# Splitting the first value product of a fused attention and SwiGLU kernel over two one-bank PSUM tiles

## The chip, the cores and the metric

The kernel runs on one core of a Trainium2 chip. A core has five engines that run side by side: PE (matrix products; PEld is its weight load), DVE (vector), ACT (scalar and activation), POOL (general purpose) and SP, which issues the DMA transfers. PE writes into PSUM, eight banks of 2 KB per partition; DVE and ACT read PSUM, all engines work on SBUF. The metric is the device time of one execution in microseconds (us), lower is better. It is given as the median of the runs; one further execution was taken with the hardware profiler and is the source of every trace row here.

## The reference

Memory attention followed by a SwiGLU feed-forward layer, in float32 (weights arrive as float64):

```python
a = softmax(phi, axis=2)                       # 8 batches, 8 heads, 576 tokens, 32 memories
k_m = einsum('bhsm,bhsd->bhmd', a, k)
v_m = einsum('bhsm,bhsd->bhmd', a, v)
attn = softmax(q @ k_m.T / 8)
x = (attn @ v_m) -> (4608, 512)                # heads side by side
xn = x / sqrt(mean(x*x) + 1e-6) * rms_g
out = (silu(xn @ w_gate) * (xn @ w_val)) @ w_out     # 512 -> 1536 -> 512
```

## The kernel before

Precision is kept by splitting a float32 operand into a rounded high part and the rest (names ending in h and l), and adding three products: high x high, high x low, low x high. A split is one ACT CAST (high) and one subtraction (low) on DVE or POOL.

The first part (until about 148 us) reduces phi, k and v to memories, computes the attention of the first two pairs of batches, and begins to convert the weights from float64. A conversion is six DVE instructions on a 128x512 tile (lines L345, L365, L347, L369, L358, L385, which write the tiles ex, mi and at last w), two ACT passes between them (L350 for ex, L376 for mi), then an ACT CAST to wh or oh (L402) and a subtraction on POOL to wl or ol (L403). A name like ex2_0 is kind 2 (w_out) of block 0; kinds 0 and 1 are w_gate and w_val.

The second part is 48 steps i, one for each pair of batches and block of 128 columns of the hidden layer. Attention and value memories are not multiplied out: each step computes

- the value product vp: the pair's value memories times the block of w_gate and w_val, 12 matmuls 128x256 (L840), in one PSUM tile with tag vw, two banks, one buffer; index cc is 0 or 1, the pair of heads;
- its evacuation: xh (ACT, L853) and xl (DVE, L854), each in two halves of 64 partitions, the second with its two blocks swapped;
- the gate and value products pg and pv (L876): xh and xl times the attention weights ath and atl, for four groups of columns, with tags g and v, two banks each;
- sg = silu(pg) on ACT (L884), hf = pv x sg on DVE (L885), the split of hf into hh (ACT) and hl (POOL);
- after every second step, the output products po (L918), 9 times 6 matmuls 128x512, tag o, two banks, added to acc on DVE (L925; the first time copied by ACT, L923).

Beside them run the conversion of the remaining weights and the attention of the last two pairs (query transposes qtp, scores S), whose PSUM tiles are also of tag o.

The order of the work: each helper returns a list of closures, each is given a number (the tables VW, GV, O, PRE, PSW, SU and others), and they are recorded in the order of the numbers. The recorded program then goes through the language's own scheduler, which reorders each engine's instructions by its own estimate of their times and sets the waits. So a small edit in one step can move instructions in later ones. The second part takes over the PSUM banks from the first; a tile waits until the last reader of its banks in the first part is done.

Of the kernel before, what the change touches and what calls it, by code (L numbers as in the profile page):

```python
# [8 lines left out]
F32 = mybir.dt.float32  # L9
# [4 lines left out]
ALU = mybir.AluOpType  # L14
# [76 lines left out]
def kernel(  # L91
# [25 lines left out]
    nc = tc.nc  # L117
    P = 128
# [309 lines left out]
    with ExitStack() as c1:  # L428
        sb = c1.enter_context(tc.tile_pool(name="sb1", bufs=2, reuse_waits="tile"))
        ps = c1.enter_context(tc.tile_pool(name="ps1", bufs=2, space=PSUM, reuse_waits="tile"))  # L430
# [330 lines left out]
        def place(base, offsets, steps):  # L761
            assert len(offsets) == len(steps)
            return [(base + o, f) for o, f in zip(offsets, steps)]
# [8 lines left out]
        for b in range(B):  # L772
# [11 lines left out]
            else:  # L784
                p0 = PRM["PH"][b - 2] + PRM["PD"][b - 2]
                ev += place(p0, PRM["PREP"], preps[b][:5])
                e = max(K_AT[b - 2] + 6 * PRM["KP"], p0 + PRM["PREP"][-1]) + PRM["EXP"][b - 2]
# [3 lines left out]
        for pr in range(G):  # L791
            for s in range(HP):
                t = PRM["S_AT"][pr * HP + s]
# [18 lines left out]
    sb = ctx.enter_context(tc.tile_pool(name="sb2", bufs=1, reuse_waits="tile"))  # L812
    ps = ctx.enter_context(tc.tile_pool(name="ps2", bufs=2, space=PSUM, reuse_waits="tile"))

    NS = (NP // G) * NU * G * 2
    vw, hsplit, accs = {}, {}, {}

    def where(i):

        ps_, r = divmod(i, NU * G * 2)  # L820
        u, r = divmod(r, G * 2)
        pi, f = divmod(r, 2)
        return ps_, u, ps_ * G + pi, 2 * u + f

    def vw_steps(i):

        ps_, u, pr, j = where(i)

        def mm(cc):
            def f():  # L830
                if cc == 0:
                    vw[i] = [ps.tile([P, 2, 2, 256], F32, tag="vw", name=f"vp{i}", bufs=1)]
                vp = vw[i][0]
                vh, vl = vm[pr][:, 0], vm[pr][:, 1]
                wh, wl = (x.rearrange("p hp g f -> p hp (g f)") for x in wsplit[ps_ * NJ + j])
                for e in range(2):
                    def lhs(vt):
                        return vt[:, cc, e].rearrange("p o x -> p (o x)")
                    for n, (l, r) in enumerate(((vh, wh), (vh, wl), (vl, wh))):
                        nc.tensor.matmul(  # L840
                            vp[:, cc, e, :], lhs(l), r[:, 2 * cc + e, :],
                            start=(n == 0), stop=(n == 2),
                        )
            return f

        def evac():
            vp = vw[i][0]
            xh = sb.tile([P, 2, 2, 256], F32R, tag="xh", name=f"xh{i}", bufs=2)
            xl = sb.tile([P, 2, 2, 256], F32R, tag="xl", name=f"xl{i}", bufs=2)
            for h in range(2):  # L850
                rows = slice(64 * h, 64 * h + 64)
                src = vp[rows, :, ::-1, :] if h else vp[rows]
                nc.scalar.copy(xh[rows], src)  # L853
                nc.vector.tensor_tensor(out=xl[rows], in0=src, in1=xh[rows].bitcast(F32), op=ALU.subtract)  # L854
            vw[i] = xh, xl
        return [mm(0), mm(1), evac]
# [78 lines left out]
    def o_tile(name):  # L935
        return ps.tile([P, 512], F32, tag="o", name=name)
# [104 lines left out]
    ev = place(-1.0, PRM["VW"], vw_steps(0))  # L1041
    for i in range(NS):
        ps_, u, pr, j = where(i)
        ev += place(i, PRM["GV"], gv_steps(i))
        if i + 1 < NS:
            ev += place(i + (PRM["VW0"] if i == 0 else 0), PRM["VW"], vw_steps(i + 1))
# [59 lines left out]
```

## Time and profile before

| | |
|---|---|
| median of 3 runs | 908.6 us (907.46 to 909.01) |
| the profiled execution, its own time | 910.09 us |
| its span, first to last instruction | 908.3 us |
| granted PE clock over the span | 0.969 |
| PE busy | 838.9 us (92%) |
| DVE busy | 592.2 us (65%) |
| ACT busy | 421.1 us (46%) |
| POOL busy | 286.6 us (32%) |

The shares are means over stages with different limits, so the prediction cuts the span into stretches. In rows of the order of time, a group of alike instructions is one row with its start and length; the brackets tell how long the engine sat idle before it and what ended that.

### The profile page before, as it was taken

How to read it: one execution, taken by the hardware profiler on the slowest of the kernel's cores; microseconds unless marked ns; L12 is line 12 of the kernel's file. 1: busy time of each engine (PE TensorE's matmuls, PEld its weight loads, DVE VectorE, ACT ScalarE, POOL GpSimd, SP SyncE). 2: the span in 40 equal slices, each digit the busy share in tenths (PEclk: the TensorE clock that was granted, in tenths of full speed). 3: DMA queues.
4: the chain of work that ended last, by engine and by line, in shares of the span. 5: the costliest groups of instructions: out<-in, count | busy, mean ns of one | idle time of the engine just before them, and what ended most of it. 6: DMA issues, size and time to landing. Idle time of an engine off the chain costs nothing.

```text
span 908.3 us, 15828 instructions
## 1 busy us (share of the span) xinstructions
PE 838.9 (92%) x6207; PEld 744.3 (82%) x6207; DVE 592.2 (65%) x1026; ACT 421.1 (46%) x717; POOL 286.6 (32%) x242
## 2 busy tenths in 40 slices
PE   4989485899989999899999999999999999999997
PEld 3777474889887899788888997798889999999996
DVE  5577968997898877988754655632445455454543
ACT  2656433777766464665543343254424333243330
POOL 3463745333333324234242241412112121121120
PEclk9889887999999999999999999999999999999999
DMA  8976543553464341634214134411204012040046
GB/s 284 324 254 236 201 157 96 182 185 86 153 166 132 106 119 61 165 110 153 89 58 140 35 94 128 97 55 47 93 1 140 1 48 93 1 140 1 1 111 144
DMA packets 81506, 106.41 MB, mean 117 GB/s; under 512 B 34324, under 2 KB 52248, under 8 KB 81432
## 3 DMA queue, kind: packets, MB, share of 16 engines
q1 hardware_dynamic: 81432, 105.41, 37.6%
q8 instruction: 49, 0.80, 0.4%
q14 instruction: 25, 0.20, 0.1%
HBM read 73.93 MB, written 31.46 MB: 116 GB/s over the span
## 4 chain that ended last, share of the span: by engine, by line
PE 74%; DVE 14%; issue 4%; DMA 4%; ACT 3%; POOL 1%; SPq 0%; DVEq 0%; ACTq 0%; POOLq 0%
PE po L918 29%; PE pv L876 14%; PE pg L876 14%; PE vp L840 7%; PE kvp L573 3%; PE xp L235 1%; DVE mi L365 1%; DVE xl L854 1%; DVE ex L345 1%; DVE w L385 1%; ACT xh L853 1%; PE qtp L685 1%; DVE mi L369 1%; DVE acc L925 1%; DMA phi<-in_phi_dram 1%
## 5 line engine op out<-in xcount | busy, mean ns | idle before, releaser
L899 POOL TENSOR_TENSOR hl<-hf,hh 128x512 fp32r<-128x512 f32 (+1 forms) x96 | 139.6, 1454 | 410.9 <-ACT hh L898 399.6
L925 DVE TENSOR_TENSOR acc<-po,acc 128x512 f32<-128x512 f32 x180 | 123.1, 687 | 130.2 <-PE po L918 129.5
L918 PE MATMUL po<-oh,hh 128*128 128x512 f32 x432 | 173.6, 403 | 3.6 <-DVE acc L925 2.6
L918 PE MATMUL po<-oh,hl 128*128 128x512 f32 x432 | 171.1, 396 | 0.0
L918 PE MATMUL po<-ol,hh 128*128 128x512 f32 x432 | 170.9, 396 | 0.0
L884 ACT ACTIVATE sg<-pg 128x256 f32<-128x256 f32 x192 | 77.7, 409 | 163.2 <-PE pg L876 144.2
L854 DVE TENSOR_TENSOR xl<-vp,xh 64x1024 fp32r<-64x1024 f32 x96 | 117.2, 1220 | 45.9 <-ACT xh L853 44.4
L885 DVE TENSOR_TENSOR hf<-pv,sg 128x256 f32<-128x256 f32 x192 | 85.3, 453 | 73.0 <-PE pv L876 51.1
L853 ACT CAST xh<-vp 64x1024 fp32r<-64x1024 f32 x96 | 96.6, 1007 | 51.7 <-PE vp L840 21.6
L898 ACT CAST hh<-hf 128x512 fp32r<-128x512 f32 (+1 forms) x96 | 64.6, 673 | 82.3 <-DVE hf L885 57.0
L918 PEld LDWEIGHTS po<-oh,hl 128*128 128x128 f32 x432 | 81.5, 189 | 19.5
L918 PEld LDWEIGHTS po<-oh,hh 128*128 128x128 f32 x432 | 81.5, 189 | 19.3 <-DVE acc L925 4.5
L876 PE MATMUL pg<-ath,xh 128*128 128x320 f32 (+1 forms) x384 | 86.6, 299 | 7.9 <-ACT xh L853 6.3
L918 PEld LDWEIGHTS po<-ol,hh 128*128 128x128 f32 x432 | 81.7, 189 | 11.5 <-DMA ol<-od 0.2
L840 PE MATMUL vp<-wh,vm 128*128 128x256 f32 x384 | 85.5, 288 | 4.8 <-DVE at L212 2.3
L876 PE MATMUL pv<-ath,xh 128*128 128x320 f32 (+1 forms) x384 | 84.7, 300 | 4.7 <-DVE hf L885 4.6
L876 PE MATMUL pg<-ath,xl 128*128 128x320 f32 (+1 forms) x384 | 85.7, 296 | 0.0
L876 PE MATMUL pv<-atl,xh 128*128 128x320 f32 (+1 forms) x384 | 84.7, 296 | 0.0
L876 PE MATMUL pg<-atl,xh 128*128 128x320 f32 (+1 forms) x384 | 84.4, 297 | 0.0
L876 PE MATMUL pv<-ath,xl 128*128 128x320 f32 (+1 forms) x384 | 83.3, 296 | 0.0
L876 PEld LDWEIGHTS pg<-ath,xh 128*128 128x128 f32 x384 | 63.8, 190 | 13.3 <-ACT xh L853 6.6
L840 PEld LDWEIGHTS vp<-wh,vm 128*128 128x128 f32 x384 | 66.0, 191 | 8.4 <-DVE xl L854 3.0
(129 smaller groups left out, 1377.5 us busy)
## 6 DMA issues: line engine op xcount, KB each, us to landing
kv<-in_k_dram SPq DMA_DIRECT2D x32, 288.0 KB, 4.8
kv<-in_v_dram SPq DMA_DIRECT2D x32, 288.0 KB, 5.4
out_dram<-acc SPq DMA_DIRECT2D x72, 128.0 KB, 2.4
raw<-in_moe_w_gate_dram SPq DMA_DIRECT2D x12, 512.0 KB, 4.8
raw<-in_moe_w_val_dram SPq DMA_DIRECT2D x12, 512.0 KB, 3.7
wd<-wh SPq DMA_DIRECT2D x12, 512.0 KB, 3.0
wd<-wl SPq DMA_DIRECT2D x12, 512.0 KB, 4.1
raw<-in_moe_w_out_dram SPq DMA_DIRECT2D x12, 512.0 KB, 3.6
```

Source lines behind the costliest of these rows:

```text
L235: nc.tensor.matmul(xp[64 * j:64 * j + 64, P * cc:P * cc + P], st["at"][:, t, cc, 64 * j:64 * j + 64], gb[:, j, cc], start=True, stop=True,)
L573: nc.tensor.matmul(kvp[64 * par:64 * par + 64, cc, 0:128], e_bd[j][:, hp, c, :], st["kv", b, hp][:, :, 64 * c:64 * c + 64], start=(c == 0) ...
L840: nc.tensor.matmul(vp[:, cc, e, :], lhs(l), r[:, 2 * cc + e, :], start=(n == 0), stop=(n == 2),)
L853: nc.scalar.copy(xh[rows], src)
L854: nc.vector.tensor_tensor(out=xl[rows], in0=src, in1=xh[rows].bitcast(F32), op=ALU.subtract)
L876: nc.tensor.matmul(pt[:, :N], l[:, cc, b, half * P:half * P + P], r[:, b, cc, t0:t0 + n, :].rearrange("p t x -> p (t x)"), start=(m == 0), ...
L884: nc.scalar.activation(sg[:, :N], pg[:, :N], AF.Silu)
L885: nc.vector.tensor_tensor(out=hf[:, :, b, :], in0=pv[:, :N].rearrange("p (t x) -> p t x", x=64), in1=sg[:, :N].rearrange("p (t x) -> p t x ...
L898: nc.scalar.copy(hh, hv)
L899: nc.gpsimd.tensor_tensor(out=hl, in0=hv, in1=hh.bitcast(F32), op=ALU.subtract)
L918: nc.tensor.matmul(po, l[:, tt, :], r, start=(m == 0), stop=(m == 5))
L925: nc.vector.tensor_tensor(out=accs[key], in0=po, in1=accs[key], op=ALU.add)
```

## The change

For step 0 alone, the value product is written into two tiles of one bank each, one for each cc, with tag o (the output products' banks). Each tile is evacuated by itself: two CASTs of 64x512, then two subtractions of 64x512. All later steps keep the two-bank tile. Three tiles that nothing uses are created first, so that tags vw, v and g keep banks ahead of o.

```diff
+    ps.tile([P, 2, 2, 256], F32, tag="vw", name="vw_first", bufs=1)
+    for t in "vg":
+        ps.tile([P, 512], F32, tag=t, name=f"{t}_first")
...
         def mm(cc):
             def f():
-                if cc == 0:
-                    vw[i] = [ps.tile([P, 2, 2, 256], F32, tag="vw", name=f"vp{i}", bufs=1)]
-                vp = vw[i][0]
+                if i == 0:
+                    vw.setdefault(i, []).append(o_tile(f"vp{i}_{cc}").rearrange("p (e f) -> p e f", e=2))
+                elif cc == 0:
+                    whole = ps.tile([P, 2, 2, 256], F32, tag="vw", name=f"vp{i}", bufs=1)
+                    vw[i] = [whole[:, 0], whole[:, 1], whole]
+                vp = vw[i][cc]
...
-                            vp[:, cc, e, :], lhs(l), r[:, 2 * cc + e, :],
+                            vp[:, e, :], lhs(l), r[:, 2 * cc + e, :],
...
         def evac():
-            vp = vw[i][0]
             xh = sb.tile([P, 2, 2, 256], F32R, tag="xh", name=f"xh{i}", bufs=2)
             xl = sb.tile([P, 2, 2, 256], F32R, tag="xl", name=f"xl{i}", bufs=2)
+            if i == 0:
+                for cc, vp in enumerate(vw[i]):
+                    halves = ((slice(0, 64), vp[:64]), (slice(64, P), vp[64:, ::-1, :]))
+                    for rows, src in halves:
+                        nc.scalar.copy(xh[rows, cc], src)
+                    for rows, src in halves:
+                        nc.vector.tensor_tensor(
+                            out=xl[rows, cc], in0=src, in1=xh[rows, cc].bitcast(F32), op=ALU.subtract
+                        )
+                vw[i] = xh, xl
+                return
+            vp = vw[i][2]
             for h in range(2):
```

In the built program the count of matmuls, DMAs and POOL instructions is unchanged; ACT has two CASTs more and DVE two subtractions more. The order differs from step 0's value product on; from step 15's gate product on it is the same again on every engine. Line numbers in the changed kernel are 5 to 20 higher.

Three places. In these rows a name carries its step or block and then a number of the program's own; x2 is two alike in a row. First ACT, just before and in step 0's evacuation: before,

```order
L350 ACTIVATE ex2_0_1828<-ex2_0_1828 128x512
L853 CAST xh0_1822<-vp0_1809 64x1024
L376 ACTIVATE mi2_0_1833<-mi2_0_1833 128x512
L853 CAST xh0_1822<-vp0_1809 64x1024
L402 CAST oh0_2027<-w2_0_1839 128x512
```

and now, up to the table load for silu:

```order
L862 CAST xh0_1826<-vp0_0_1812 64x512 x2
L350 ACTIVATE ex2_0_1836<-ex2_0_1836 128x512
L862 CAST xh0_1826<-vp0_1_1819 64x512 x2
L376 ACTIVATE mi2_0_1841<-mi2_0_1841 128x512
L402 CAST oh0_2035<-w2_0_1847 128x512
L873 CAST xh1_1901<-vp1_1849 64x1024
L904 ACT_TABLE_LOAD
```

The first tile's two CASTs moved ahead of ex2_0, and step 1's first CAST ahead of the table load. Second DVE at the same place: before,

```order
L369 SCALAR_TENSOR_TENSOR mi2_0_1833<-raw_20_1724,mi2_0_1833 128x512
L358 SCALAR_TENSOR_TENSOR ex2_0_1828<-raw_20_1724,ex2_0_1828 128x512
L854 TENSOR_TENSOR xl0_1823<-vp0_1809,xh0_1822 64x1024
L385 TENSOR_TENSOR w2_0_1839<-mi2_0_1833,ex2_0_1828 128x512
L345 TENSOR_SCALAR ex2_1_1969<-raw_21_1741 128x512
L365 TENSOR_SCALAR mi2_1_1980<-raw_21_1741 128x512
L854 TENSOR_TENSOR xl0_1823<-vp0_1809,xh0_1822 64x1024
```

and now:

```order
L369 SCALAR_TENSOR_TENSOR mi2_0_1841<-raw_20_1724,mi2_0_1841 128x512
L864 TENSOR_TENSOR xl0_1827<-vp0_0_1812,xh0_1826 64x512 x2
L358 SCALAR_TENSOR_TENSOR ex2_0_1836<-raw_20_1724,ex2_0_1836 128x512
L864 TENSOR_TENSOR xl0_1827<-vp0_1_1819,xh0_1826 64x512 x2
L385 TENSOR_TENSOR w2_0_1847<-mi2_0_1841,ex2_0_1836 128x512
```

The subtractions of the first tile stand ahead of ex2_0's last pass, those of the second ahead of w2_0. Third ACT again, at the silu of steps 1 and 2: before,

```order
L853 CAST xh2_1974<-vp2_1917 64x1024
L402 CAST wh2_2074<-w0_2_2068 128x4x128
L402 CAST wh2_2074<-w1_2_2151 128x4x128
L884 ACTIVATE sg1_00_1966<-pg1_00_1952 128x256
L884 ACTIVATE sg1_01_2002<-pg1_01_1988 128x256
```

and now the same place, which ends with the weights' CAST,

```order
L873 CAST xh2_1982<-vp2_1925 64x1024
L904 ACTIVATE sg1_00_1974<-pg1_00_1960 128x256
L904 ACTIVATE sg1_01_2010<-pg1_01_1996 128x256
L402 CAST wh2_2082<-w0_2_2076 128x4x128
L873 CAST xh2_1982<-vp2_1925 64x1024
```

where silu moved ahead of the weights' CASTs; and some rows later in the changed kernel

```order
L402 CAST wh2_2082<-w1_2_2159 128x4x128
L873 CAST xh3_2147<-vp3_2041 64x1024
L350 ACTIVATE ex0_3_2237<-ex0_3_2237 128x512
L904 ACTIVATE sg2_00_2134<-pg2_00_2120 128x256
L376 ACTIVATE mi0_3_2242<-mi0_3_2242 128x512
```

where ex0_3 moved directly ahead of step 2's first silu (before, the copy acc0_0 stood there).

## The prediction

> **What bounds the kernel now.** I read the share of each engine by stage first, then the chain of waits, then the order of time around the first step. By stage (columns: stretch and its length, then the busy time of PE, PEld, DVE, ACT and POOL, then PEclk, DMA share, GB/s):
>
> ```profile
> 146.00:165.00 19.00, 10.38 (x57) 10.08 (x58) 18.64 (x24) 11.35 (x21) 11.79 (x10) 0.64 0.67 204
> 165.00:226.00 61.00, 56.87 (x428) 51.58 (x427) 52.87 (x83) 44.24 (x79) 22.12 (x15) 1.00 0.46 135
> 226.00:352.00 126.00, 119.59 (x813) 106.04 (x812) 103.26 (x168) 76.90 (x127) 42.65 (x31) 1.00 0.42 124
> 352.00:575.00 223.00, 214.33 (x1470) 187.36 (x1469) 159.32 (x299) 103.98 (x178) 70.53 (x58) 1.00 0.36 108
> ```
>
> From 165 us on PE is the bound: 56.87 of 61.00, 119.59 of 126.00 and so on. The 19 us before that, where step 0 of the second part begins, belong to DVE (18.64 of 19.00) while PE idles 8.6 us. The chain of waits there (start, length, what):
>
> ```profile
> 146.23 1.69 DVE w L385
> 148.25 1.09 DVE ex L345
> 149.34 1.41 DVE mi L365
> 150.76 1.40 DVE ex L347
> 152.16 1.67 DVE mi L369
> 153.83 0.86 DVE ex L358
> 154.69 1.14 DVE xl L854
> 155.86 1.02 ACT xh L853
> 156.92 1.22 PE pg L876 x4
> ```
>
> Weight conversion on DVE, then one half of step 0's xl, then the second half of xh, and only then PE. The order of time shows why (start, length, engine, line, operation; in brackets the idle time and what ended it):
>
> ```profile
> 148.31 0.39 PE L840 MATMUL vp<-wh,vm 128*128 128x256 f32 x1 [2.34 <-DVE at L212]
> 148.48 0.49 ACT L223 CAST ath<-at 128x128 fp32r<-128x128 f32 x2
> 152.19 0.63 ACT L350 ACTIVATE ex<-ex 128x512 int32<-128x512 int32 x1 [3.22 <-DVE ex L347]
> 152.73 0.99 ACT L853 CAST xh<-vp 64x1024 fp32r<-64x1024 f32 x1
> 154.62 1.21 DVE L854 TENSOR_TENSOR xl<-vp,xh 64x1024 fp32r<-64x1024 f32 x1
> 155.75 0.67 DVE L385 TENSOR_TENSOR w<-mi,ex 128x512 f32<-128x512 f32 x1
> 155.86 1.01 ACT L853 CAST xh<-vp 64x1024 fp32r<-64x1024 f32 x1 [1.30 <-DVE xl L854]
> 156.92 0.79 PE L876 MATMUL pg<-ath,xh 128*128 128x256 f32 x2 [6.32 <-ACT xh L853]
> ```
>
> ACT has nothing to do from 148.97 to 152.19, because the ex that it must do first waits for DVE, and xh stands behind it. PE then waits 6.32 us, its longest wait in the second part.
>
> **The restart of PE.** Now vp0 is two tiles in banks that wait for nobody, so it starts where PE's work before it ends (148.31 less 2.34, near 146.0); both tiles are done before ACT is free, so this alone gives nothing. The planner has put the two CASTs of the first tile ahead of ex: they run from 148.97. A 64x512 CAST is in no trace; half of the 64x1024 one is 0.50 us, and a 128x512 pass of ACT (ex) takes 0.63. I take 0.55, nearer the half, as operation and source are the same. So the first tile's xh is there at 150.1, and four products run on PE in the hole. The second tile's CASTs follow ex, at 152.73, until 153.85: PE restarts there and not at 156.92, 3.0 us earlier. What is late next is xl: its first half now follows mi on DVE (ends 153.83). A 64x512 subtraction costs between half of 1.21 and the 0.67 of w; I take 0.65, nearer the half with an overhead, so two end at 155.15 and PE, three products on, waits 0.6 us. The added work is four pieces for two on each engine: 4 x 0.55 - 2.00 = 0.2 us of ACT, hidden in its hole, and 4 x 0.65 - 2.42 = 0.2 us of DVE, contained in these times.
>
> **What is left of it at the next barrier.** Until the query transposes, PE then has 13 products, 11 matmuls of vp1 and 4 products of xl's second tile. Their pitch depends on the granted clock:
>
> ```profile
> 145.70:149.10 3.40, 1.06 (x14) 0.92 (x12) 3.40 (x4) 3.01 (x8) 3.40 (x4) 1.00 0.25 78
> 149.10:162.75 13.65, 7.33 (x35) 7.04 (x34) 13.32 (x18) 6.40 (x9) 7.82 (x7) 0.50 0.71 208
> 155.90:159.35 3.45, 2.43 (x11) 2.43 (x12) 3.35 (x6) 1.75 (x3) 1.29 (x1) 0.50 0.94 229
> 159.35:162.75 3.40, 3.40 (x18) 3.40 (x17) 3.17 (x7) 2.45 (x4) 0.62 (x1) 0.50 1.06 353
> 159.85 0.85 PE pv L876 x4
> 163.34 0.71 PE vp L840 x6
> ```
>
> At 0.50 four take 0.85 us (0.215 each), at 1.00 six take 0.71 (0.12). The clock came back after the first slice that PE filled (159.35 on). With PE busy from 155.2 on, the slice from 155.90 is the full one and the clock is back at 159.35, one slice earlier. So: 13 x 0.215 from 155.2 to 158.0; six of vp1 to 159.35, five more to 159.9; four of xl to 160.4. Then ACT sets the time:
>
> ```profile
> 162.01 1.28 ACT L884 ACT_TABLE_LOAD   x1
> 163.31 0.66 ACT L884 ACTIVATE sg<-pg 128x256 f32<-128x256 f32 x2
> 164.24 0.54 PE L876 MATMUL pg<-ath,xh 128*128 128x320 f32 x2
> ```
>
> The next pg (four time columns, t0 = 4 on, 164.24) needs sg to free its bank. On ACT xh1 now stands ahead of the table load: 159.95 + 1.0 + 1.28 + 0.4 gives 162.7, pg at 162.8. Of 3.0 us there remain **1.4**.
>
> **From 165 to 226 us.** PE's waits before, between 148 and 226 us (engine line <- releaser: total, times, longest):
>
> ```profile
> PE pg L876 <- ACT xh L853: 6.3, 1, 6.3
> PE vp L840 <- DVE at L212: 2.3, 1, 2.3
> PE pv L876 <- DVE hf L885: 1.9, 2, 1.0
> PE pg L876 <- ACT sg L884: 1.5, 1, 1.5
> PE qtp L964 <- ACT acc L923: 0.7, 1, 0.7
> DVE mx L992 <- PE S L982: 5.4, 1, 5.4
> ```
>
> The last three of PE, 4.1 us, are later than step 0, and the new order meets them: ahead of step 1's last hf stand 23 conversion instructions on DVE since 148 us, where 32 stood, and on ACT sg1_00 follows xh2 directly, where two wh CASTs stood between, the second of which needs a w from DVE. Against it: DVE has no slack here, and what is put off must be done. All 4.1 gone is one end, nothing gone or the 1.4 lost as well the other. I take **1.2**: the 1.5 of sg, less 0.3 for later conversions. The cover of the conversions is wide: DVE waits 5.4 us for PE's S near 222, so it had caught up by then. If that were used up, each would add its own 0.67 or so to PE's path.
>
> **The rest.** Up to step 15 of 48, where the third stretch ends, the order differs from before in many places, without a direction that I can read: PE waits 6.4 us there (126.00 - 119.59). I take **0**, with half of that, 3.2, as bound on either side. From there on all five engines have the same rows in the same order, and a shift stays: 0. On SP three of the q loads pass a weight load; that weight is read later as well, so 0, and nothing of PE waits for a DMA in the waits above. PE's matmuls are the same in number and shape.
>
> **Sum:** -1.4 - 1.2 = -2.6 us. The profiled execution took 910.09 us (span 908.3 and 1.8 around it), so 907.5 in its own terms. It lies 1.5 above the median of 908.6, so the median comes to **906.0**.
>
> **Rivals.** (a) *DVE takes it back; no change.* For it: 18.64 of 19.00 and 52.87 of 61.00 busy, and the first 3.0 us already shrink to 1.4. Against: the 5.4 us of DVE's slack. The 1.4 shrinks to about 0.6: 908.0.
>
> (b) *The clock never falls; faster.* The slice in which it was lost had PE busy 1.06 of 3.40; with vp0 starting at once it has about 2. Then 19 matmuls before 159.35 (13 and 6) run 0.095 faster, 1.8 us, and pg comes 3.2 earlier: 904.2. Against: the following slice holds some 0.6 us of PE work, less than the 1.06 with which the clock went.
> The Trainium skill, "TensorE: Matmul & The Clock Gate", section "What's actually happening", says that the clock is taken after an idle window of about 3.4 us; no window would be wholly idle now, so by that rule it would stay. The row with 1.06 us busy disagrees, and I follow the row.
>
> (c) *ACT stands in front of PE at step 2; slower.* On ACT ex0_3 now stands just ahead of sg2_00, and needs DVE's ex; pg2_10 on PE needs sg2_00's bank.
>
> ```profile
> ACT ex L350 <- DVE ex L347: 10.7, 5, 3.2
> 175.31 0.42 DVE L347 TENSOR_SCALAR ex<-ex 128x512 int32<-128x512 int32 x1
> 175.33 3.23 POOL L403 TENSOR_TENSOR wl<-w,wh 128x512 fp32r<-128x512 f32 x2 [2.12 <-ACT wh L402]
> 175.64 1.77 DVE L369 SCALAR_TENSOR_TENSOR mi<-raw,mi 128x512 f32<-128x512 uint32 x1
> ```
>
> ACT has waited for that up to 3.2 us, and beside POOL a conversion takes 1.77 us. Before, such a wait cost PE nothing. Two waits of 3.2 us on PE, here and at one later step of the same pattern, would make -2.6 + 6.4 = +3.8 with nothing hidden; I halve the second, as some work is queued on PE: +2.2, 910.8. It decides once PE's new waits behind sg exceed 2.6 + 1.8 = 4.4 us. Against: only at some of the steps does ex stand there.
> The Trainium skill, "SBUF — State Buffer", section "Who interferes with whom", has a DVE instruction with two SBUF inputs blocked for the whole of a GpSimd one; the 1.77 agrees. By it (c) would grow with every subtraction of POOL that meets ex.
>
> **How the numbers follow.** Main case 0.52, (a) 0.23, (b) 0.08, (c) 0.17. Within 0.2%, 1.8 us, a measurement of this kernel can hardly tell a change. The main case's own range is 903.1 (1.4 and all 4.1) to 907.4; a tenth of it lies within 0.2%. Faster: 0.47 + 0.08 = 0.55; same: 0.23 + 0.05 = 0.28; slower 0.17. The range goes from 902.4 (903.1 less a little of the 3.2) to 910.0, which leaves out the upper part of (c).
>
> **What would show it.** The wait of pg for xh (6.32) falls to about 3.3 and pg restarts near 153.9; clock 0.50 for two slices, not four; sg first at about 162.3; the sg wait of 1.5 gone; PE's busy share in 165 to 226 higher. Wrong would be a longer sum of PE waits from 165 to 352 than 10.5 us (4.1 and 6.4), a new wait behind sg above all.

## The result, and the profile after

The changed kernel takes 915.09 us (median of 5 runs, 912.55 to 916.53), the kernel before 908.6: 1.006 times, 95% interval 1.0037 to 1.0083. It is slower by about 6 us (5.5 by the ratio, 6.5 by the medians); the forecast was 2.6 us faster, 906.0, with a range of 902.4 to 910.0. The profiled execution took 914.7 us (span 912.9).

What the split was said to do at step 0, it does. In the order of time of the changed kernel (start, length, engine, line, operation; in brackets the idle time and what ended it):

```profile
146.89 1.17 ACT L862 CAST xh<-vp 64x512 fp32r<-64x512 f32 x2
148.11 0.39 PE L896 MATMUL pg<-ath,xh 128*128 128x256 f32 x1 [1.09 <-ACT xh L862]
151.76 1.38 DVE L864 TENSOR_TENSOR xl<-vp,xh 64x512 fp32r<-64x512 f32 x2
152.07 0.58 PE L896 MATMUL pg<-ath,xh 128*128 128x256 f32 x1 [3.22 <-ACT xh L862]
160.61 0.56 PE L896 MATMUL pg<-ath,xh 128*128 128x320 f32 x2 [1.89 <-ACT sg L904]
```

The wait of 6.32 us has become one of 1.09 and one of 3.22. The time is lost later. By stage (stretch, its length, then busy time of PE, PEld, DVE, ACT and POOL, PEclk, DMA share, GB/s):

```profile
146.00:165.00 19.00, 12.05 (x70) 11.07 (x71) 17.53 (x22) 12.16 (x22) 8.70 (x8) 0.82 0.59 184
165.00:226.00 61.00, 56.69 (x418) 50.24 (x417) 57.59 (x86) 43.32 (x76) 24.36 (x17) 1.00 0.46 137
226.00:352.00 126.00, 116.07 (x777) 102.13 (x777) 104.02 (x166) 74.15 (x124) 39.57 (x29) 0.99 0.42 124
```

Ahead of 165 us PE is busy 1.7 us longer than before, at a clock of 0.82 for 0.64; but from 226 to 352 it waits 9.9 us where it waited 6.4. What PE waits for from 160 to 352 us in the changed kernel (engine line <- releaser: total, times, longest):

```profile
PE pg L896 <- ACT sg L904: 4.9, 5, 1.9
PE po L938 <- DVE acc L945: 3.1, 3, 1.5
PE vp L849 <- DVE xl L874: 2.2, 2, 1.6
PE pv L896 <- DVE hf L905: 1.7, 1, 1.7
PE po L938 <- ACT acc L943: 1.5, 3, 1.1
```

The sum of waits from 165 to 352 us is 4.3 + 9.9 = 14.2 us. The prediction had named 10.5 as the mark above which it would be wrong, and a new wait behind silu (sg) as the likeliest reason. The longest wait for sg in this list is the one at step 0's barrier, 160.61; from 165 us on sg has 3.0 us (1.5 before), and the waits of po for acc, by DVE and ACT together, 4.6 (1.9 before). Silu is one of many.

Where in time the lead turned into a loss is seen by ACT's table loads, four of which are shown; they stand at nearly the same places of the program in both kernels. The last work of PE before the change, rp, serves as the zero. Before:

```profile
143.25 1.09 PE L204 MATMUL rp<-ident,rinv 128*128 128x128 f32 x8 [1.97 <-DVE rinv L276]
201.58 1.28 ACT L1000 ACT_TABLE_LOAD   x1
226.68 1.28 ACT L1000 ACT_TABLE_LOAD   x1
291.36 1.28 ACT L1000 ACT_TABLE_LOAD   x1
381.73 1.28 ACT L1000 ACT_TABLE_LOAD   x1
```

and after:

```profile
141.23 1.09 PE L204 MATMUL rp<-ident,rinv 128*128 128x128 f32 x8 [1.97 <-DVE rinv L276]
195.65 1.28 ACT L1020 ACT_TABLE_LOAD   x1
223.75 1.28 ACT L1020 ACT_TABLE_LOAD   x1
293.03 1.28 ACT L1020 ACT_TABLE_LOAD   x1
386.82 1.28 ACT L1020 ACT_TABLE_LOAD   x1
```

Counted from rp, the second load comes 58.33 us later before and 54.42 after: a lead of 3.9 us. At the next it is 83.43 against 82.52, a lead of 0.9; then 148.11 against 151.80, 3.7 behind; then 238.48 against 245.59, 7.1 behind, and so it stays to past 560 us; at the end it is 6.6. (The 2.0 us by which rp itself came earlier are chance: up to step 0's value product the two programs have the same rows in the same order. They are why the two profiled executions differ by 4.6 us and not by 6.6.)

Counted on PE, between the same two products in both kernels, the loss has two parts. (Columns as in the stages above; each window counts a few matmuls more that lap over its ends.) From the first pg of step 3 to that of step 5, and from there to the first pg of step 16, before:

```profile
197.07:223.01 25.94, 25.94 (x190) 23.94 (x186) 19.37 (x33) 19.98 (x34) 7.44 (x5) 1.00 0.40 111
223.01:400.33 177.32, 167.25 (x1174) 147.62 (x1172) 149.35 (x242) 107.33 (x178) 62.33 (x44) 1.00 0.43 127
```

and after:

```profile
191.10:219.52 28.42, 27.56 (x187) 24.07 (x186) 28.03 (x46) 22.71 (x39) 9.45 (x6) 1.00 0.52 147
219.52:405.41 185.89, 170.05 (x1173) 149.10 (x1172) 153.42 (x244) 107.28 (x178) 60.79 (x44) 0.99 0.42 124
```

The first part is 2.5 us long, with DVE busy for 28.03 of 28.42 us. The second is 8.6 us: PE idles 15.8 us where it idled 10.1, and its busy time for the same products is 2.8 us longer. Some 1.7 of these 2.8, by estimate, are the clock: the changed kernel has one slice of 3.41 us at 0.50 there (289.70, shown below), half of which is lost if PE is full; the kernel before has none (1.00 in its row).

One place where PE waits, near 295 us: the last of a row of nine po, which takes over a bank that a sum to acc frees. Before:

```profile
292.12 0.68 DVE L925 TENSOR_TENSOR acc<-po,acc 128x512 f32<-128x512 f32 x1
292.92 0.44 PE L918 MATMUL po<-oh,hh 128*128 128x512 f32 x1
293.37 0.75 DVE L1005 TENSOR_REDUCE sm<-ex 128x18 f32<-128x576 f32 x1
```

after:

```profile
295.04 0.75 DVE L1025 TENSOR_REDUCE sm<-ex 128x18 f32<-128x576 f32 x1 [0.34 <-ACT ex L1020]
295.71 0.68 DVE L945 TENSOR_TENSOR acc<-po,acc 128x512 f32<-128x512 f32 x1
296.45 0.50 PE L938 MATMUL po<-oh,hh 128*128 128x512 f32 x1 [1.48 <-DVE acc L945]
```

The sum to acc, which frees the bank, stood ahead of sm (and of a conversion's w) and now stands behind them; PE waits 1.48 us, where it waited for nothing.

The order of the built program, laid beside the times of the trace, gives one more number: how many conversion instructions DVE has done behind the same number of its other instructions. For the order of before, all conversions ahead of the next other instruction are counted, so each difference is the most that can be put off there.

| us in the changed kernel | 155 | 186 | 206 | 220 | 250 | 270 | 281 | 300 |
|---|---|---|---|---|---|---|---|---|
| after | 28 | 51 | 66 | 81 | 98 | 117 | 117 | 134 |
| in the order of before | 38 | 62 | 79 | 81 | 104 | 117 | 122 | 134 |
| put off | 10 | 11 | 13 | 0 | 6 | 0 | 5 | 0 |

Counted in the traces at the other instructions themselves, the difference is 7 to 12 from 161 to 208 us, 0 to 1 from 220 to 226, and between -3 and 5 from there to 352.

### The profile page after: what moved, and what is told of

The parts are those of the page before. It is cut to its first block, busy times and chain, and to the rows that moved or that the text cites. A ratio compares the mean times of both kernels' runs of the same rounds, so it can differ in the third digit from the quotient of the medians.

```text
span 912.9 us, 15844 instructions
## 1 busy us (share of the span) xinstructions
PE 837.6 (92%) x6207; PEld 740.8 (81%) x6207; DVE 600.1 (66%) x1028; ACT 421.2 (46%) x719; POOL 284.6 (31%) x242
## 4 chain that ended last, share of the span: by engine, by line
PE 64%; DVE 20%; issue 5%; ACT 5%; DMA 4%; POOL 1%; SPq 0%; DVEq 0%; ACTq 0%; POOLq 0%
PE po L938 26%; PE pv L896 12%; PE pg L896 12%; PE vp L849 6%; PE kvp L573 3%; DVE xl L874 2%; DVE ex L345 2%; DVE mi L365 2%; DVE mi L369 2%; DVE ex L358 2%; DMA phi<-in_phi_dram 2%; DVE w L385 1%; PE xp L235 1%; DVE ex L347 1%; DVE acc L945 1%
## 5 line engine op out<-in xcount | busy, mean ns | idle before, releaser
L874 DVE TENSOR_TENSOR xl<-vp,xh 64x1024 fp32r<-64x1024 f32 x94 | 114.7, 1220 | 47.9 <-ACT xh L873 46.4
L873 ACT CAST xh<-vp 64x1024 fp32r<-64x1024 f32 x94 | 94.6, 1006 | 47.0 <-PE vp L849 22.4
```

## The experiments

Two theories stood at the start: O, the loss is in the new order; S, the split or its banks cost it by themselves. Each ratio below is to runs of the kernel before on the same chip beside the experiment's own (their medians were 908.2 to 909.6 us), with its 95% interval. All experiments pin the order: a table of numbers holds the order of each engine's instructions, and each instruction is tied to the one ahead of it on its engine, without a wait. No run pins a kernel to its own order with nothing else changed; that pinning costs little is seen in split_old_rest2 (+0.2%) and split_new_to_221 (-0.3%) below.

```diff
     for _, f in sorted(ev, key=lambda e: e[0]):
         f()
+    pin_order(tc)
...
+def pin_order(tc):
...
+    for e, runs in json.loads(zlib.decompress(base64.b85decode(ORDER))).items():
+        seq = [mine[e][a + k] for a, n in runs for k in range(n)]
+        for a, b in zip(seq, seq[1:]):
+            tc.add_manual_dep(b, a.name, info, reason="pin_order")
```

So the split and the order can be had apart, and a kernel can follow one order up to a time of a trace and the other from there on. In the entries below, "ORDER" tells what the table holds.

### Split or order

```diff
 # the changed kernel
+ORDER = all engines: after until 158 us, then before; SP: after until its 233rd transfer
```

> The changed kernel (step 0 split, tags in the same banks), with the order of every engine pinned: as in the changed kernel up to 158 us of its trace, where step 0's evacuation is done, and from there on the remaining instructions in the order of the kernel before. Theory O (the loss is in the new order of steps 1 to 15, not in the split): 905 to 909 us, because PE restarts some 3 us earlier but meets the old order's barriers behind conversions, and the 5 us lost between 200 and 300 us are not lost. Theory S (the split, or the other PSUM banks, cost the time by themselves): 913 to 916 us, as the changed kernel.

Measured: 926.16 us, ratio 1.0176 (1.0151 to 1.02). Outside both theories, and by an error of the mixture: SP's queue had kept the new order for much longer than the engines. In its chain of waits (start, length, what):

```profile
187.08 0.39 SPq L412
187.53 0.55 SPq L973
188.18 6.90 DMA raw<-in_moe_w_out_dram
```

A load of w_out stood behind a store of converted weights (L412) and loads of q (L973); the conversion that needs it stood ahead of an hf, and PE waited 8.12 us for that hf, until 196.32. For the split this says nothing; it shows what one transfer out of turn costs.

```diff
 # the kernel before
+ORDER = all engines: before until 160 us, then after; SP: before until its 233rd transfer
```

> The kernel before (step 0 whole), pinned: its own order up to 160 us of its trace, then the remaining instructions in the order of the changed kernel. Theory O: 912 to 919 us; the order alone makes it slower than before, with no earlier restart of PE to set against it. Theory S: 907 to 910 us, as before.

Measured: 918.17 us, 1.0096 (1.0079 to 1.0112). As theory O, but with the same uneven cut on SP (its trace shows no wait for a load). Both were run again with SP cut over at the same point as the rest.

> As split_old_rest, but with SP's queue in the order of before too (there it stood in the order of the changed kernel, and one load of w_out was issued 8 us late behind other transfers). What is left of the change is the split of step 0 and some 20 matmuls that follow it. Theory O (the new order of steps 1 to 15 cost the time): 904 to 909 us, a part of the earlier restart and nothing lost. Theory S (the split or the banks by themselves): 913 to 918 us.

Measured: 910.17 us, 1.0018 (1.0004 to 1.0032): theory O. The split alone neither costs the 5 us nor brings anything. Its early restart ends at silu, ahead of whose table load the old order has three ACT passes of w_out's second block. In the order of time (the same columns as above):

```profile
141.97 1.97 PE L204 MATMUL rp<-ident,rinv 128*128 128x128 f32 x8 [1.97 <-DVE rinv L276]
151.60 0.47 PE L896 MATMUL pg<-ath,xh 128*128 128x256 f32 x1 [1.12 <-ACT xh L862]
163.07 0.90 PE L896 MATMUL pg<-ath,xh 128*128 128x320 f32 x2 [1.83 <-ACT sg L904]
```

The second tile's pg comes 9.6 us after rp's start (13.7 before, for the whole xh); the pg behind silu 21.1 us after it, and 21.0 before. (Ahead of that, PE also waits 3.22 us for a load of q, until 160.61.)

> As whole_new_rest, with SP's queue in the order of the changed kernel as well: step 0 whole as before, all the rest in the new order. Theory O: 912 to 919 us, as slow as the changed kernel or slower by the earlier restart that it lacks. Theory S: 906 to 910 us. If SP's order alone made whole_new_rest slow: 906 to 911 us.

Measured: 916.82 us, 1.0106 (1.0081 to 1.0131): theory O. **The new order alone, with step 0 whole, makes the kernel slower by 1.1%.** The stretch from 221 to 305 us (columns as in the stages above), first of the kernel before:

```profile
221.00:305.00 84.00, 77.59 (x552) 67.60 (x551) 74.89 (x122) 55.79 (x93) 33.14 (x23) 1.00 0.49 146
```

of the changed kernel:

```profile
221.00:305.00 84.00, 73.84 (x483) 63.52 (x484) 71.56 (x113) 54.52 (x89) 29.11 (x22) 0.98 0.47 144
```

of split_old_rest2:

```profile
221.00:305.00 84.00, 77.60 (x551) 67.82 (x546) 75.49 (x122) 55.99 (x94) 32.80 (x23) 1.00 0.48 146
```

and of whole_new_rest2:

```profile
221.00:305.00 84.00, 73.32 (x496) 62.97 (x495) 71.60 (x113) 53.40 (x87) 29.09 (x22) 0.98 0.46 141
```

PE's busy time is 77.6 in the old order and 73.3 to 73.8 in the new, with or without the split. From the first pg of step 5 to that of step 16, split_old_rest2 takes 177.30 us and whole_new_rest2 185.82: the times of the two kernels whose order they have (177.32 and 185.89).

### Up to where the new order may go

```diff
 # the changed kernel
+ORDER = all engines: after until T, then before
```

Theory D, in what follows, is that the loss is a debt: conversions that the new order puts off on DVE and that must be done later. T = 190 and 245 us, with SP in the new order until its 233rd transfer:

> The changed kernel with its own order up to 190 us of its trace, and from there on the remaining instructions in the order of the kernel before. In the changed kernel PE was 6.2 us ahead at 185 us, some 2 of them from before the change. Theory O: the lead is kept in part, 903 to 908 us, and the conversions that the new order had put off are caught up in the order of before. Theory S: 913 to 916 us.

Measured: 920.63 us, 1.0116 (1.0097 to 1.0136), outside both theories; SP's uneven cut shows again, as DVE waits 4.5 us for a load of w_val.

> The changed kernel with its own order up to 245 us of its trace, then the order of before. By then PE had given back 5 of the 10 us that it lost between 185 and 305 us. Theory O: between the run with 190 us and the changed kernel, 907 to 912 us. Theory S: 913 to 916 us.

Measured: 911.93 us, 1.003 (1.0016 to 1.0044), inside theory O's range.

T = 190, 163, 206 and 221 us, with SP cut over at the same point:

> As split_new_to_190, with SP's queue cut over at the same point. Theory O: 903 to 908 us, the lead of some 4 us that the changed kernel had at 185 us kept, and none of the loss after it. If the loss is the debt of conversions put off before 190 us, which any order must pay: 910 to 915 us. Theory S: 913 to 917 us.

Measured: 913.89 us, 1.0064 (1.0044 to 1.0085): the debt. Twelve conversion instructions stand in a row on DVE from 187.40 to 195.32 us, and behind them an hf. PE's first long wait after the cut:

```profile
195.89 0.80 PE L896 MATMUL pv<-ath,xh 128*128 128x256 f32 x2 [4.71 <-DVE hf L905]
```

> The changed kernel with its own order up to 163 us of its trace (step 1's first CAST ahead of the table load for silu, so PE passes that point 4 us earlier), then the order of before on all engines. Seven to eight conversion instructions are put off by then (some 5 us of DVE), and the old order asks for them at once. Theory D: they come in front of step 1's hf, the lead of 4 us is given back within 15 us, 907 to 912 us. If PE's early restart could be kept beside the old order: 904 to 907 us. Theory S (the split itself costs): 913 to 918 us.

Measured: 910.21 us, 1.0016 (0.9997 to 1.0035), as theory D says.

> The changed kernel with its own order up to 206 us of its trace, then the order of before on all engines, SP's queue too. At that point 13 DVE conversion instructions, some 8 us, are put off against the order of before, the largest debt there is, and the old order asks for them at once. Theory D: 911 to 917 us. Theory N (the loss comes from the new order after 206 us, which is gone here): 903 to 908 us.

Measured: 914.44 us, 1.005 (1.0032 to 1.0067): theory D, again with a wait for hf behind the conversions that had been put off:

```profile
212.64 0.51 PE L896 MATMUL pv<-ath,xh 128*128 128x256 f32 x2 [4.47 <-DVE hf L905]
```

> The same with 221 us, where the changed kernel has no DVE conversion put off any more (81 done, 81 in the order of before at the same place) and PE is still some 3 us ahead, a part of it from before the change. Theory D: nothing is left to pay and the lead stays, 904 to 908 us, the fastest of all orders so far. If the loss needs another cause, or the mixture of two orders costs by itself: 909 to 915 us.

Measured: 907.4 us, 0.9971 (0.9952 to 0.999): theory D, and **the fastest of all that do the whole work, 0.3% faster than the kernel before**. In 15 us of new order between the last two cuts the debt falls from 13 instructions, by the table's count, to none, and the time falls by 7 us. From 221 to 305 us it has the old PE time again:

```profile
221.00:305.00 84.00, 77.60 (x518) 67.58 (x517) 74.40 (x121) 54.19 (x91) 30.47 (x22) 1.00 0.52 155
```

So the changed kernel, which is the same up to 221 us, loses some 8 us by the order that follows (915.1 against 907.4).

### Debt of conversions, or order of the other work

```diff
 # conv_new: the kernel before; conv_old: the changed kernel
+ORDER = own order; each conversion instruction behind as many others as in the other kernel
```

> The kernel before (step 0 whole) with every engine pinned to its own order, save the conversion of the weights (its DVE, ACT and POOL instructions and its loads and stores): each of these stands behind as many other instructions of its engine as in the changed kernel. PE's order is that of before, row for row. Up to 13 DVE conversion instructions, some 8 us, are put off between 155 and 210 us. Theory D (the loss is the debt of the conversions put off, paid between 200 and 300 us): 913 to 919 us. Theory N (the loss is in the new order of the other work, PE's products and ACT's silu and copies): 906 to 911 us.

Measured: 918.08 us, 1.0084 (1.0065 to 1.0103): as theory D says. With the conversions placed as in the new order the loss is there, though PE's order is untouched. (That a mixture can lose merely by being one, the next run shows.)

> The changed kernel (step 0 split) pinned to its own order, save the conversion of the weights, each instruction of which stands behind as many other instructions of its engine as in the kernel before. PE's order is that of the changed kernel, row for row. Theory D: 904 to 910 us, no debt, and at most a part of the early restart kept. Theory N: 913 to 918 us.

Measured: 926.79 us, 1.0184 (1.0166 to 1.0202): neither theory. Conversions at their old places amid the other work's new order are worse than either order whole; PE waits 4.4 us for a silu near 166 us and 4.8 us for a qT near 264 us, both on ACT.

```diff
 # both kernels, own ORDER pinned (the first two blocks of w_gate and w_val keep all 512 columns)
+            c = 512 if kind < 2 and n < 2 else 32
             V.scalar_tensor_tensor(
-                out=ex, in0=d["raw"][:, :, 1], scalar=-(1 << 31), in1=ex,
+                out=ex[:, :c], in0=d["raw"][:, :c, 1], scalar=-(1 << 31), in1=ex[:, :c],
...
-                out=mf, in0=d["raw"].bitcast(U32)[:, :, 0], scalar=2.0 ** -32, in1=m,
+                out=mf[:, :c], in0=d["raw"].bitcast(U32)[:, :c, 0], scalar=2.0 ** -32, in1=m[:, :c],
```

> The kernel before with its own order pinned, but in the conversion of all weights from block 2 on and of all of w_out, the two DVE instructions at L358 and L369 work on 32 of 512 columns: they leave out the sign and the low 32 bits of the other columns, which takes some 1.4 us of DVE from each conversion. It is the base for after_light; by itself 900 to 909 us (in its trace PE waited 10.5 us between 165 and 352 us, and a part of that was DVE's).

Measured: 898.41 us, 0.9878 (0.9848 to 0.9908). This kernel and the next leave out the sign and the low 32 bits of most columns of the weights.

> The changed kernel with its own order pinned and the same two instructions shortened. Theory D (the debt of conversions on a DVE without room): the order no longer costs, and the early restart of PE counts: 0 to 4 us faster than before_light. Theory N (the order of the other work, PE's products and ACT's silu and copies, which stays the same here): 4 to 7 us slower than before_light, as without the shortening.

Measured: 902.5 us, 0.9929 (0.9903 to 0.9955), 4.1 us above before_light. That speaks against theory D as it was put: the shortening makes both kernels over 10 us faster, and the new order still costs about as much (the two intervals leave 1 to 8 us). From the first pg of step 5 to that of step 16, before_light:

```profile
220.47:393.04 172.57, 165.45 (x1174) 147.63 (x1172) 135.62 (x243) 106.84 (x179) 60.51 (x44) 1.00 0.42 130
```

and after_light:

```profile
214.74:392.38 177.64, 166.64 (x1174) 147.53 (x1172) 135.43 (x241) 106.69 (x179) 60.00 (x44) 1.00 0.42 127
```

PE idles 7.1 and 11.0 us there, a difference of 3.9, against 5.8 without the shortening (10.1 and 15.8). The new order still costs 5.1 us of the 8.6, and neither profile has a slice at 0.50 in this stretch. DVE is idle for 37 and 42 us of it, so it is not its total that binds, but what stands in front of what. The part ahead of it is another matter: from the first pg of step 3 to that of step 5 the new order took 28.42 us for 25.94, and with the shortening it takes 25.81 for 25.93. That first loss of 2.5 us is the debt, and it goes when DVE has room.

### Which engine's order

```diff
 # the changed kernel
+ORDER = pe_new_221: after until 221 us, then before, PE after throughout
+ORDER = pe_old_221: after, PE before from 221 us on
```

> As split_new_to_221 (the order of before from 221 us on), but PE keeps the order of the changed kernel throughout. Theory V (the loss comes from the order on DVE, ACT and POOL, not from PE's): 904 to 910 us, as split_new_to_221. Theory P (PE's new order costs it): 911 to 917 us.

Measured: 922.47 us, 1.0146 (1.0123 to 1.0168): against theory V, but worse than P allows too.

> The reverse: the changed kernel, with PE alone in the order of before from 221 us on. Theory V: 912 to 919 us, as the changed kernel. Theory P: 904 to 910 us.

Measured: 918.99 us, 1.0114 (1.0092 to 1.0136): as V, which the run before this one rules out. Taken together: a PE order of the one kind with the others of the other kind is worse than either kind whole, so the two runs can't tell whether the loss is in PE's queue or in the four others.

In urgent_first the table of DVE changes at eight places such as this one near 260 us; in urgent_late sums and halves of xl move the other way in the old order.

```diff
 L358 ex2_5
+L945 acc0_0
 L385 w2_5
 L345 ex0_6
 L365 mi0_6
-L945 acc0_0
```

> The changed kernel with its own order pinned, save that on DVE, between 221 and 303 us, eight instructions for which PE waits (four sums to acc and four halves of xl) move ahead of the one to three conversion instructions that stand directly before them, 16 places in all. Theory U (of the loss after 221 us the most comes from such instructions that stand behind conversions on DVE): 909 to 913 us. If where they stand doesn't matter: 914 to 917 us.

Measured: 917.81 us, 1.0092 (1.0071 to 1.0112): theory U fails. To move these four sums and four halves of xl ahead brings nothing.

> The kernel before with its own order pinned, save that on DVE, between 223 and 300 us, nine such instructions (six sums to acc and three halves of xl) move behind the one or two conversion instructions that follow them, 14 places in all, some 10 us of DVE time, of which PE would wait for a part. Theory U: 911 to 916 us. If where they stand doesn't matter: 907 to 910 us.

Measured: 915.8 us, 1.0062 (1.0041 to 1.0082): as U. To move nine instructions by one or two places each in the old order costs as much as the whole change did. The two together say that the old order can easily be spoilt on DVE, and that the new one isn't mended by these eight moves.

## Why the prediction was wrong, point by point

**The restart of PE: right.** The two CASTs of the first tile run in ACT's hole; the four pieces take 1.17 and 1.38 us a pair, 0.585 and 0.69 each (0.55 and 0.65 estimated). PE's wait is 3.22 us (about 3.3 said), and PE restarts at 152.07, or 154.1 with the 2.0 us of chance added (153.9 said). The clock stands at 0.50 for two slices and not four:

```profile
146.34:149.75 3.41, 1.12 (x5) 0.72 (x5) 3.41 (x3) 1.71 (x5) 3.41 (x3) 1.00 0.57 190
149.75:156.58 6.83, 4.39 (x19) 4.10 (x20) 6.68 (x10) 2.96 (x5) 2.81 (x4) 0.50 0.60 145
```

**What is left at the next barrier: right.** The pg behind silu starts 160.61 - 141.23 = 19.38 us after rp, before 164.24 - 143.25 = 20.99: a gain of 1.6 us (1.4 said). It is not the split's own, though: split_old_rest2 has the split without the new order, and gains nothing there.

**From 165 to 226 us, -1.2: wrong.** The lead did grow, to 3.9 us at the second table load, by the mechanism named: conversions put off, silu earlier. At 223.75 it is 0.9, 0.7 us less than at the barrier. Two of the signs named failed too: the wait of 1.5 us for sg fell to 0.93 and did not go, and PE's busy time is 56.69 of 61.00 us and not above 56.87. The step that failed here is the cover: "The cover of the conversions is wide", because DVE waited 5.4 us for S near 222. The new order uses that cover up. DVE is busy 57.59 of 61.00 us where it was busy 52.87, and by 220 us it has made good all 13 instructions; PE loses 2.5 us meanwhile, and loses nothing when the conversions are shortened (after_light).

**"The rest ... I take 0", bound 3.2: the step that failed.** It cost 8.0 us: from 0.9 ahead to 7.1 behind (8.6 counted on PE, of which 5.8 are waits and 2.8 a longer busy time, 1.7 of that by estimate the clock). In the terms of the sum: -1.4 - 1.2 + 0 was said, and -1.6 + 0.7 + 8.0 was measured, 7.1. A reordering "without a direction that I can read" was priced at nothing, with half of PE's own waits as its bound, as if PE's waits could only be shared out anew. But the waits that an order leaves aren't a pool that bounds what another order can cost. Of the 16 experiments in which steps 0 to 15 ran in another order than the old one with the conversions whole, 15 had a ratio above 1, from 1.0016 (whose interval alone reaches below 1) to 1.0184; the cut at 221 us was the one below. What the prediction had counted and set aside, 23 conversion instructions where 32 stood on an engine with 5.4 us to spare, points at the loss ahead of 224 us; behind it, where most was lost, nothing was owed.

**The rivals.** (a) had the right thing for the wrong price: DVE did take most of the lead back by 224 us, but that was not the end of it. (b) did not happen: the slice ahead of the loss had PE busy 1.12 of 3.41 us, and the clock went. By the rule of the Trainium skill cited there ("TensorE: Matmul & The Clock Gate", "What's actually happening"), which asks for an idle window, it would have stayed; the row disagrees again. The same happened a second time in the changed kernel, after two of its waits (0.60 us for acc, 1.57 for xl):

```profile
286.29:289.70 3.41, 1.43 (x22) 1.29 (x23) 3.32 (x6) 0.47 (x1) 0.00 (x0) 1.00 0.97 189
289.70:293.11 3.41, 3.41 (x13) 3.02 (x13) 3.30 (x8) 1.75 (x4) 1.07 (x1) 0.50 0.78 287
```

(c) had the right sign. Its place was wrong, as there is no wait at step 2's first silu, but sg has more waits than before (4.9 us for 1.5 from 160 to 352 us, of which 1.9 are at step 0's barrier). That is 3.4 new ones, below the 4.4 at which (c) was to decide; the waits of po for acc have 2.7 more.

**What stays open.** Shown: the loss is in the order and not in the split, all of the loss against the kernel before lies after 221 us, and it is there with and without the split. Not shown: which pairs of instructions make it up. The debt of DVE explains the loss ahead of 221 us and the runs cut at 190 and 206 us, but DVE's room doesn't decide after 221 us (after_light). Which queue carries the loss is open: pe_new_221 and pe_old_221 lose by being mixtures, and urgent_first moves eight instructions only. Nor is it shown how much of each run's loss is the clock: in the profiled executions whole_new_rest2, urgent_first and urgent_late have one slice at 0.50 between 165 and 400 us, conv_new two, pe_new_221 and pe_old_221 three each, and split_new_to_221 none. That acc stood behind w and sm near 295 us is one instance in the trace, no proof of the cause.

## What to carry to other kernels

Where a scheduler sits between the source and the queues, split an edit's price in two: the edit with the order held, and the new order with the edit left out; here the first was +0.2% and the second +1.1%. A reordering of a fitted program is no zero with a symmetric bound: count what it puts off against the engine's slack, and lean to a loss (15 of 16 here). And where it goes wrong, look for the point at which nothing is owed: to keep the new order up to there and the old one behind it made the only version faster than both, by 0.3%.

## What the runs showed of the hardware

- The clock fell after slices of 3.41 us in which PE was partly busy. The kernel before has a slice at the same place of the program as the changed kernel's at 286.29, with 1.87 us of PE work in it for 1.43, and its clock stayed:

```profile
285.63:289.04 3.41, 1.87 (x27) 1.69 (x26) 3.32 (x6) 0.22 (x1) 0.00 (x0) 1.00 0.81 169
```

In the 20 profiled executions, between 145 and 890 us, the clock fell after slices with at most 1.85 us of PE work (pe_old_221 from 382.3 on), and stayed after slices with at least 1.6 (pe_old_221 from 256.0 on); between these it did either. By estimate a fall costs 1.7 us more, half of the next slice, if PE is full in it.
- A conversion on DVE cost more in the new order with the same instructions: between 146 and 352 us the means of its six passes add up to 4.81 us, before to 4.52. Not each rose (L365 fell from 712 to 679 ns, L385 from 962 to 835). The two that rose most (count, busy us, mean ns), before:

```profile
L345 DVE TENSOR_SCALAR ex<-raw 128x512 int32<-128x512 int32 x22 | 14.6, 662 | 0.4
L347 DVE TENSOR_SCALAR ex<-ex 128x512 int32<-128x512 int32 x22 | 11.8, 538 | 0.0
```

after:

```profile
L345 DVE TENSOR_SCALAR ex<-raw 128x512 int32<-128x512 int32 x22 | 18.3, 831 | 0.4
L347 DVE TENSOR_SCALAR ex<-ex 128x512 int32<-128x512 int32 x22 | 14.9, 677 | 0.0
```

One instance stands beside a subtraction on POOL, 1.78 us for an instruction that takes 0.42 alone:

```profile
298.03 1.56 POOL L919 TENSOR_TENSOR hl<-hf,hh 128x640 fp32r<-128x640 f32 x1 [1.16 <-ACT hh L918]
298.08 1.78 DVE L347 TENSOR_SCALAR ex<-ex 128x512 int32<-128x512 int32 x1
```

The Trainium skill, "SBUF — State Buffer", section "Who interferes with whom", has this for DVE instructions with two SBUF inputs and for some with one that run in a mode with two ports; its list of the latter has tensor_scalar. L347 is one, with one input, and the row agrees; no run here shows the mode that it ran in.
- The same first part of the program (to 140 us) ran up to 5.2 us earlier in one profiled execution (rp at 138.03 in split_new_to_221) than in that of before (143.25), as its clock slices fell: the granted clock up to rp was 0.90 there and 0.87 here, over the same matmuls. A trace's own time is not its kernel's median: that run took 904.21 us, the median is 907.4.
